# A retention recurrence and a gated feed-forward layer: order of the first chunk's transposes, second weight slices in halves, two states in a row

## The chip, the cores and the metric

The kernel runs on one core of a Trainium2 chip. The metric is the device time of the program in microseconds (us). Three runs of the kernel before took 225.05 to 225.13 us, with a median of 225.07 us. The profile is one execution of the same program; the span in it is 223.4 us, and all times "at" which something happens are counted from the start of that span. The TensorE clock that was granted is 1.0 throughout.

## The reference

For each of 4 batches and 8 heads a state of 64 x 64 decays and collects outer products, token by token, and the output of a token is its q times that state. The outputs of the 8 heads side by side are the 512 features x of a token. 3072 tokens then go through a gated feed-forward layer with 1536 hidden features:

```
for t in range(768):
    state = gamma * state + outer(k[t], v[t])      # per batch and head, gamma = 1 - 2**(-5-h)
    y[t]  = scale * q[t] @ state
x   = y as (4*768 tokens, 512)
out = (sigmoid(x @ w_gate) * (x @ w_val)) @ w_out
```

## The kernel before

**Chunks and tiles.** The 768 tokens are cut into 6 chunks of 128. One chunk of all 4 batches is a tile `t` of 512 columns for the feed-forward layer. Within a chunk the recurrence is worked out in closed form: scores (k times q), times a decay mask, times v; plus the q times the state that the chunks before have left. The attention works on pairs of batches: index `i` is chunk `i // 2`, pair `i % 2`, and `j` is the batch within the pair. "The last chunk" of the change's title means the last batch of the first token chunk, `(i, j) = (1, 1)`; "the third" is `(1, 0)`.

**Order.** The order on each engine is the order in which the code emits instructions (`manual_schedule`). The code first emits the loads of the first tile, then constants, then the head: the first tile's attention, with groups of matmuls on zeros in between (`keep_on`), then the first tile's feed-forward layer, then a loop over tiles 1 to 5 in which attention steps of later tiles are placed among groups of matmuls by a table, `plan`.

**Loads.** k, q, v and all weights are loaded by GpSimd's DMA queue, one instruction for each, in the order of the code; GpSimd also computes (`first_scaled`, line 371, `later_tables`, lines 182 and 184, `scale_k`, line 225), in the same order. `kf` and `qf`, the first batch's k and q, come over two other queues. Each of GpSimd's loads counts on one of 8 semaphores in turn, so a load is issued only when the one eight before it has landed. A weight slice `s` holds 256 of the 1536 hidden columns, that is two groups `n1 = 2s, 2s + 1` of 128. `load_w` (line 82) loads a slice whole (256 KB) or some of its 4 groups `kk` of 128 rows; the first slices of gate (`wg`) and val (`wv`) come in halves of rows, the others whole.

**The head.** `first_transpose(i, j, which, eng)` transposes k (`which` 0) or q (1) of one batch on TensorE and lets `eng` (ScalarE `act` or VectorE `dve`) copy it from PSUM to `kqT` (lines 348 and 349). `first_scores` (lines 233 and 355) multiplies them and masks the product on VectorE with `decay`, two instructions. `first_y` (lines 365 and 368) multiplies the masked scores by v and copies the result to `xT`. `exps_y(p)` (line 156) makes a quarter of `taby`, a table for later tiles, on ScalarE; it reads `col` and `lgz`, which VectorE makes (lines 159 and 153).

**The first feed-forward tile.** `first_parts` (line 410) computes two groups `n1` of gate or val, rows `kk` 0 and 1 of both groups first, then 2 and 3, so that it can begin with half a slice. `up_part` (line 392) computes one group with its four `kk` in a row. `gate_times_val` applies the sigmoid on ScalarE (line 420) and multiplies on VectorE (line 421). `first_state(i)` (line 379) forms the state of a pair from the scaled k (`ks`) and v, 16 matmuls of 64 columns in two halves of TensorE.

**Later tiles.** `xbar(i)` (line 220) transposes a pair's k and q by DMA from the queue of SyncE into `kqX`. `hold(i)` (line 540) is a tiny copy on GpSimd that waits for such a transpose, so that the loads behind it are not issued earlier. `block(old, new, st)` does one pair's outputs, the next one's scores and a state: `inter` (line 272), `quarter_scores` (line 249), `intra` (line 279), `state` (line 302). All matmul results use one ring of 8 PSUM banks (`bank`): the n-th result waits for the reader of the one eight before it.

Of the kernel before, what the change touches and what calls it, by code (L numbers as in the profile page):

```python
# [11 lines left out]
ALU = mybir.AluOpType  # L12
# [3 lines left out]
def kernel(  # L16
# [12 lines left out]
    nc = tc.nc  # L29
# [3 lines left out]
    C = 128  # L33
# [18 lines left out]
    def half(e):  # L52
        return slice(e * D, (e + 1) * D)
# [22 lines left out]
    wg = wpool.tile([128, KT, D_FF], BF16, name="wg")  # L76
    wv = wpool.tile([128, KT, D_FF], BF16, name="wv")
    wo = wpool.tile([128, NFF, D_MODEL], BF16, name="wo")

    def load_w(dst, w, s, kk=slice(0, KT)):  # L80
        cols = slice(s * 256, (s + 1) * 256)
        nc.gpsimd.dma_start(out=dst[:, kk, cols], in_=w.rearrange("(kk p) n -> p kk n", p=128)[:, kk, cols])  # L82

    def load_gate_val(s):
        load_w(wg, moe_w_gate, s)
        load_w(wv, moe_w_val, s)
# [7 lines left out]
    def first(dst, x, b, n, eng):  # L94
        eng.dma_start(out=dst, in_=x[b:b + n, :, 0:C, :].rearrange("b h s d -> s (b h) d"))  # L95
# [8 lines left out]
    def entry(t, j):  # L104
        return t[:, j * H:(j + 1) * H, :]
# [4 lines left out]
    ahead = const.tile([128, C], F32, name="ahead")  # L110
    first(entry(kn[0], 1), k, 1, 1, nc.gpsimd)
    nc.gpsimd.iota(ahead, pattern=[[-1, C]], base=0, channel_multiplier=1, allow_small_or_imprecise_dtypes=True)  # L112
    for x, b in ((q, 1), (k, 2), (q, 2), (k, 3), (q, 3), (v, 0), (v, 1), (v, 2), (v, 3)):
        tiles = kn if x is k else qn if x is q else vs
        first(entry(tiles[b // 2], b % 2), x, b, 1, nc.gpsimd)
    for dst, w in ((wg, moe_w_gate), (wv, moe_w_val)):
        load_w(dst, w, 0, slice(0, 2))
        load_w(dst, w, 0, slice(2, 4))
    load_gate_val(1)
    load_gate_val(2)  # L120


# [2 lines left out]
    nlg = const.tile([128, 2, NP], F32, name="nlg")  # L125
    lgz = const.tile([128, 2, NP], F32, name="lgz")
    lsc = const.tile([128, 1], F32, name="lsc")
    tok = const.tile([128, NT], F32, name="tok")
    col = const.tile([128, C], F32, name="col")
# [10 lines left out]
    nc.vector.memset(lsc, math.log(scale))  # L140
    for h in range(H):
        nc.vector.memset(nlg[:, h % 2, h // 2:h // 2 + 1], -lg[h])
    nc.vector.tensor_scalar(ident, ahead, 0.0, None, op0=ALU.is_equal)
    nc.vector.scalar_tensor_tensor(causal, ahead, -1.0e6, ahead, op0=ALU.mult, op1=ALU.min)
    for e in range(2):
        nc.vector.tensor_tensor(decay[:, e], causal.unsqueeze(1).to_broadcast([128, NP, C]),
                                nlg[:, e].unsqueeze(2).to_broadcast([128, NP, C]), op=ALU.mult)
        nc.scalar.activation(decay[:, e], decay[:, e], AX.Exp, bias=lsc)
    nc.vector.tensor_copy(entry(kn[0], 0), kf)
    nc.scalar.copy(entry(qn[0], 0), qf)  # L150
    for e in range(2):
        for j in range(2):
            nc.vector.tensor_scalar(lgz[half(e), j], nlg[half(e), e ^ j], -1.0, None, op0=ALU.mult)

    def exps_y(p):
        nc.scalar.activation(taby[:, p], col, AX.Exp, bias=lsc, scale=lgz[:, 0, p:p + 1])

    def later_constants():
        nc.vector.tensor_scalar(col, ahead, ahead[:, 0:1], -1.0, op0=ALU.subtract, op1=ALU.mult)
        for t in range(NT):  # L160
            nc.vector.tensor_scalar(tok[:, t:t + 1], ahead[:, 0:1], float(t * C), None, op0=ALU.add)

# [11 lines left out]
    def last_constants():  # L174
        nc.vector.tensor_scalar(causal, ahead, 0.0, None, op0=ALU.is_le)

    def later_tables():
        src = tabs.rearrange("s (p e) t -> s e t p", e=2)
        dst = tabsk.rearrange("s t j (p e) -> s j e t p", e=2)
        for j in range(2):  # L180
            for e in range(2):
                nc.gpsimd.tensor_copy(dst[:, j, e], src[:, e ^ j])
        for e in range(2):
            nc.gpsimd.tensor_tensor(maskk[:, e], causal.unsqueeze(1).to_broadcast([128, NP, C]),
                                    tabsk[:, 0, e, 0::2].unsqueeze(2).to_broadcast([128, NP, C]), op=ALU.mult)
# [5 lines left out]
    def zero_scores():  # L191
        for r in range(2):
            for j in range(2):
                for e in range(2):
                    nc.vector.memset(sts[r][j][e][half(1), :, 0:D], 0.0)
# [5 lines left out]
    def bank(shape, dt=F32):  # L201
        return pf.tile(shape, dt, tag="ff", name="ff")

    def heads(t, j, p):
        return t[:, j * H + 2 * p:j * H + 2 * p + 2, :].rearrange("s h d -> s (h d)")
# [80 lines left out]
    def x_of(t, kk, lo=0, hi=512):  # L286
        per = NP // len(xT[t])
        return xT[t][kk // per][:, kk % per, lo:hi]
# [17 lines left out]
    def new_za(i):  # L306
        za[i] = at.tile([128, 2, NP, D], F32, tag="za", name="za", bufs=4)
# [36 lines left out]
    def first_transpose(i, j, which, eng):  # L344
        x = (kn[i], qn[i])[which]
        tp = bank([128, NP, C], BF16)
        for p in range(NP):
            nc.tensor.transpose(tp[:, p, :], heads(x, j, p), ident)
        eng(kqT[i][:, which, j], tp)

    def first_scores(i, j):
        scores(i, j)
        for e, st in enumerate((stA, stB)):
            st[i, j] = at.tile([128, NP, C], BF16, tag=f"sf{e}", name=f"sf{e}", bufs=4)
            nc.vector.tensor_tensor(st[i, j], sc[i, j][e], decay[:, e], op=ALU.mult)
# [17 lines left out]
    def first_state(i):  # L373
        z = bank([128, 2, NP, D])
        for j in range(2):
            for p in range(NP):
                for e in range(2):
                    n = j * H + 2 * p + e
                    nc.tensor.matmul(z[half(e ^ j), j, p, :], ks[i][:, n, :], vs[i][:, n, :],  # L379
                                     start=(j == 0 and p == 0), stop=True, skip_group_check=True)  # L380
        new_za(i)
        nc.vector.tensor_copy(za[i], z)
# [11 lines left out]
    def up_part(t, w, n1s, lo=0, hi=512):  # L394
        n = hi - lo
        u = bank([128, 512])
        for i, n1 in enumerate(n1s):
            for kk in range(KT):
                product(t > 0, u[:, i * n:(i + 1) * n], w[:, kk, n1 * 128:(n1 + 1) * 128], x_of(t, kk, lo, hi),
                        start=(kk == 0), stop=(kk == KT - 1))  # L400
        return u[:, :len(n1s) * n]

    def first_parts(w, cuts):

        us = [bank([128, 512]) for _ in range(2)]
        for lo, hi in zip((0, *cuts), (*cuts, 512)):
            for k0 in (0, 2):
                for n1, u in enumerate(us):
                    for kk in range(k0, k0 + 2):
                        nc.tensor.matmul(u[:, lo:hi], w[:, kk, n1 * 128:(n1 + 1) * 128], x_of(0, kk, lo, hi),  # L410
                                         start=(lo == 0 and kk == 0), stop=(kk == KT - 1), skip_group_check=True)
        return us

    def gate_times_val(t, n1s, lo, hi, ps):
        n = hi - lo
        if t not in hT:
            hT[t] = ffn.tile([128, NFF, 512], BF16, tag="hT", name="hT", bufs=2)
        gs = ffn.tile([128, 512], F32, tag="gs", name="gs")
        g = gs[:, :len(n1s) * n]
        nc.scalar.activation(g, ps[0], AX.Sigmoid)  # L420
        nc.vector.tensor_tensor(hT[t][:, n1s[0]:n1s[-1] + 1, lo:hi], g.rearrange("p (i n) -> p i n", n=n),  # L421
                                ps[1].rearrange("p (i n) -> p i n", n=n), op=ALU.mult)
# [39 lines left out]
    def keep_on(n):  # L462
        u = bank([128, 512])
        for _ in range(n):
            nc.tensor.matmul(u, zero[:, :128], zero, start=True, stop=True)  # L465
# [3 lines left out]
    act, dve = nc.scalar.copy, nc.vector.tensor_copy  # L469

    new_kqT(0)
    new_kqT(1)
    keep_on(11)
    first_transpose(0, 0, 0, dve)
    first_transpose(0, 0, 1, act)
    later_constants()
# [1 line left out]
    first_scores(0, 0)  # L478
    more_constants()
    first_transpose(0, 1, 1, act)  # L480
    exps_y(0)
    first_transpose(1, 0, 0, act)
    exps_y(1)
    keep_on(1)
    first_scores(0, 1)
    first_transpose(1, 0, 1, act)
    exps_y(2)
    exps_y(3)
    keep_on(2)
    first_scores(1, 0)  # L490
    first_transpose(1, 1, 0, act)
    later_exps()
    first_transpose(1, 1, 1, dve)
    keep_on(2)
    first_y(0, 0, (act, act))
    first_scores(1, 1)
# [11 lines left out]
    first_scaled(1, 1, entry(kn[1], 1))  # L508
    load_gate_val(4)
    load_gate_val(5)  # L510
    for n1, ps in enumerate(zip(first_parts(wg, (3 * C,)), first_parts(wv, ()))):
        gate_times_val(0, (n1,), 0, 512, ps)
    for n1 in (2, 4):
        gates = [up_part(0, wg, (n1 + i,)) for i in range(2)]
        for i in range(2):
            gate_times_val(0, (n1 + i,), 0, 512, (gates[i], up_part(0, wv, (n1 + i,))))
        if n1 == 2:
            last_constants()
            zero_scores()
            later_tables()  # L520
        first_state(n1 // 2 - 1)
    load_out(0)
    load_out(1)
    load_kq(2)
# [105 lines left out]
```

## Time and profile before

| What | Value |
|---|---|
| time, median of three runs | 225.07 us (225.05 to 225.13) |
| span of the profiled run | 223.4 us |
| TensorE busy | 216.9 us, 97% |
| VectorE busy | 122.9 us, 55% |
| ScalarE busy | 70.2 us, 31% |
| GpSimd busy | 105.5 us, 47% |
| GpSimd's DMA queue (q0) | 80928 packets, 13.90 MB |

The engines are named PE (TensorE matmul), PEld (TensorE weight load), DVE (VectorE), ACT (ScalarE), POOL (GpSimd) and SP (SyncE). A line number such as L392 is that of the kernel's text, and can be the line of a helper that many steps share. A row of a timeline has the start, the time, the engine, the line, the operation, what is written and read, and the count; behind it stands how long the engine had been idle and what ended that. [...]consecutive matmuls overlap, so how fast TensorE goes is read from the distance of starts, not from durations.

Of the three parts of the head, by the profile's stretches: from 5.80 to 15.30 us TensorE is busy for 7.66 of 9.50 us, from 15.30 to 19.10 for 3.64 of 3.80 us, and from 19.10 to 27.00 for 7.84 of 7.90 us.

### The profile page before, as it was taken

To read this page: it belongs to the slowest core of one execution; us is meant where nothing else is said; L and a number is where in the kernel's file an instruction comes from. 1 tells how busy PE (TensorE), PEld (TensorE's weight loads), DVE (VectorE), ACT (ScalarE), POOL (GpSimd) and SP (SyncE) were. 2 spreads that over 40 slices of the span, in tenths; PEclk is the share of its full clock that TensorE was granted. 3 is DMA by queue.
4 is the path that set the end of the run, shared out by engine and by line. 5 is a ranking of instruction groups with operands and counts; after the bars stand their busy time and mean duration, and the time that the engine had idled before them with its cause. 6 is when DMAs were issued, how large, how long until landed. Compare 5 with 4: busy or idle time off the path is not lost.

```text
span 223.4 us, 6386 instructions
## 1 busy us (share of the span) xinstructions
PE 216.9 (97%) x2764; PEld 127.5 (57%) x2770; DVE 122.9 (55%) x243; ACT 70.2 (31%) x121; POOL 105.5 (47%) x128
## 2 busy tenths in 40 slices
PE   7799999999999999999999999999999999999994
PEld 2554444559999566556556556555555555555554
DVE  5862853094994885755916645925644922333301
ACT  5774232334233212332222332321332322333221
POOL 7999996878975916709367082640000000000000
PEclk9999999999999999999999999999999999999999
DMA  9999999999999999999999989896600012100022
GB/s 133 146 166 192 191 186 173 175 145 270 136 138 149 127 119 205 160 86 81 122 122 173 170 52 135 85 131 123 141 3 0 3 47 97 47 4 0 4 94 94
DMA packets 105788, 25.84 MB, mean 116 GB/s; under 512 B 94752, under 2 KB 102816, under 8 KB 105760
## 3 DMA queue, kind: packets, MB, share of 16 engines
q0 software_dynamic: 80928, 13.90, 85.3%
q1 hardware_dynamic: 23648, 11.21, 26.1%
q8 instruction: 21, 0.34, 0.6%
q10 hardware_dynamic: 1184, 0.33, 0.6%
q14 instruction: 7, 0.06, 0.1%
HBM read 28.31 MB, written 6.29 MB: 155 GB/s over the span
## 4 chain that ended last, share of the span: by engine, by line
PE 90%; POOL 5%; DMA 3%; issue 0%; DVE 0%; POOLq 0%
PE ff L392 82%; DMA wg<-in_moe_w_gate_dram 3%; PE ff L279 3%; PE ff L249 2%; POOL vs L95 2%; PE ff L272 2%; POOL kn L95 1%; POOL qn L95 1%; PE ff L302 1%; POOL wg L82 1%; POOL wv L82 1%; PE ff L214 0%; PE ff L379 0%; DVE ob L458 0%; POOL ahead L112 0%
## 5 line engine op out<-in xcount | busy, mean ns | idle before, releaser
L421 DVE TENSOR_TENSOR hT<-gs,ff 128x512 bf16<-128x512 f32 x72 | 48.6, 685 | 52.9 <-PE ff L392 49.9
L392 PE MATMUL ff<-xT,wg 128*64 128x512 bf16 (+2 forms) x616 | 71.9, 346 | 0.1
L392 PE MATMUL ff<-xT,wv 128*64 128x512 bf16 (+2 forms) x614 | 71.7, 346 | 0.1
L420 ACT ACTIVATE gs<-ff 128x512 f32<-128x512 f32 x72 | 42.9, 597 | 83.1 <-PE ff L392 82.7
L392 PE MATMUL ff<-wo,hT 128*64 128x512 bf16 (+3 forms) x580 | 64.6, 361 | 0.1
L392 PEld LDWEIGHTS <-wv 128*64 128x64 bf16 (+1 forms) x616 | 36.2, 109 | 24.4
L392 PEld LDWEIGHTS <-wg 128*64 128x64 bf16 (+1 forms) x616 | 35.5, 109 | 24.3 <-DMA wg<-in_moe_w_gate_dram 0.6
L392 PEld LDWEIGHTS <-hT 128*64 128x64 bf16 (+1 forms) x582 | 32.7, 109 | 27.1
L262 DVE TENSOR_TENSOR st<-ff,maskk 128x256 bf16<-128x256 f32 (+2 forms) x76 | 35.1, 492 | 7.5 <-PE ff L249 6.5
L442 ACT COPY ob<-ff 128x512 f32<-128x512 f32 x23 | 13.5, 585 | 57.0 <-PE ff L392 56.9
L295 DVE TENSOR_TENSOR xT<-ff,taby 128x512 bf16<-128x512 f32 x20 | 12.9, 685 | 23.7 <-PE ff L279 23.7
L540 POOL COPY held<-kqX 128x1 bf16<-128x1 bf16 x7 | 1.3, 184 | 34.9 <-DMA kqX<-qn 33.0
L225 POOL TENSOR_TENSOR ks<-kn,tabsk 128x1024 bf16<-128x1024 bf16 x8 | 15.5, 1942 | 1.6 <-PE ff L392 1.2
L70 POOL DMA_DIRECT2D qn<-in_q_dram x20 | 15.4, 795 | 0.0
L70 POOL DMA_DIRECT2D kn<-in_k_dram x20 | 15.2, 769 | 0.0
L60 POOL DMA_DIRECT2D vs<-in_v_dram x10 | 12.1, 1205 | 1.1 <-DMA wo<-in_moe_w_out_dram 1.0
L66 POOL DMA_DIRECT2D kn<-in_k_dram x10 | 9.3, 929 | 1.8 <-issue 1.7
L66 POOL DMA_DIRECT2D qn<-in_q_dram x10 | 9.2, 917 | 0.0
L465 PE MATMUL ff<-zero 128*128 128x512 bf16 x19 | 7.6, 527 | 1.2 <-DVE zero L139 1.2
L315 DVE TENSOR_TENSOR zb<-za,tabz 128x512 bf16<-128x512 f32 x10 | 8.2, 827 | 0.0
L279 PE MATMUL ff<-st,vs 128*64 128x128 bf16 x160 | 6.4, 222 | 0.0
L458 DVE COPY ob<-ff 128x256 f32<-128x256 f32 (+1 forms) x2 | 0.7, 357 | 9.2 <-PE ff L392 9.2
(74 smaller groups left out, 117.5 us busy)
## 6 DMA issues: line engine op xcount, KB each, us to landing
out_dram<-ob SPq DMA_DIRECT2D x23, 256.0 KB, 2.9
vs<-in_v_dram POOLq DMA_DIRECT2D x10, 256.0 KB, 7.5
kn<-in_k_dram POOLq DMA_DIRECT2D x13, 128.0 KB, 4.6
qn<-in_q_dram POOLq DMA_DIRECT2D x13, 128.0 KB, 4.6
wo<-in_moe_w_out_dram POOLq DMA_DIRECT2D x4, 384.0 KB, 7.0
wg<-in_moe_w_gate_dram POOLq DMA_DIRECT2D x5, 256.0 KB, 6.3
wv<-in_moe_w_val_dram POOLq DMA_DIRECT2D x5, 256.0 KB, 6.8
kn<-in_k_dram POOLq DMA_DIRECT2D x20, 64.0 KB, 4.0
```

The costliest lines, as they stand in the source:

```text
L60: nc.gpsimd.dma_start(out=vs[i], in_=v[2 * h:2 * h + 2, :, t * C:(t + 1) * C, :].rearrange("b h s d -> s (b h) d"))
L66: nc.gpsimd.dma_start(out=tiles[i][:, 0:H], in_=src[0])
L70: nc.gpsimd.dma_start(out=dst[:, e], in_=pairs[:, 1 - e])
L95: eng.dma_start(out=dst, in_=x[b:b + n, :, 0:C, :].rearrange("b h s d -> s (b h) d"))
L225: nc.gpsimd.tensor_tensor(ks[i], kn[i], tabsk[:, i // 2].rearrange("s j h -> s (j h)").unsqueeze(2) .to_broadcast([C, 2 * H, D]), op=ALU.mult)
L262: nc.vector.tensor_tensor(st[i, j][to, :, n], sc[i, j][e][of, :, n], maskk[to, e ^ j, :, n], op=ALU.mult)
L279: nc.tensor.matmul(y[i, j][half(e), p, :], vs[i][:, j * H + 2 * p + e, :], st[:, p, :], start=False, stop=True, skip_group_check=True)
L295: nc.vector.tensor_tensor(xT[t][0][:, :, c:c + C], y[i, j], taby, op=ALU.mult)
L392: nc.tensor.matmul(o[c], w[:, c], x, **marks)
L420: nc.scalar.activation(g, ps[0], AX.Sigmoid)
L421: nc.vector.tensor_tensor(hT[t][:, n1s[0]:n1s[-1] + 1, lo:hi], g.rearrange("p (i n) -> p i n", n=n), ps[1].rearrange("p (i n) -> p i n", n ...
L442: nc.scalar.copy(ob, o)
```

## The change

It has three parts.

1. *Head.* The k of the last batch is transposed ahead of the third batch's scores, not after them, so that its eviction doesn't stand in line with that of q; the eviction of its q moves from VectorE, where it comes after four masks, to ScalarE. To make room on ScalarE the four `exps_y` are spread differently, the first of them ahead of all evictions, for which VectorE makes `lgz` and `col` earlier.
2. *Weights.* The second slices of gate and val are loaded in halves of rows, like the first ones, and the groups 2 and 3 that use them go through `first_parts`, whose matmuls need only half a slice to begin.
3. *States.* The two `first_state` groups, which stood after groups 3 and 5, come one after the other after group 5.

```diff
--- before.py
+++ after.py
@@ -113,10 +113,10 @@
     for x, b in ((q, 1), (k, 2), (q, 2), (k, 3), (q, 3), (v, 0), (v, 1), (v, 2), (v, 3)):
         tiles = kn if x is k else qn if x is q else vs
         first(entry(tiles[b // 2], b % 2), x, b, 1, nc.gpsimd)
-    for dst, w in ((wg, moe_w_gate), (wv, moe_w_val)):
-        load_w(dst, w, 0, slice(0, 2))
-        load_w(dst, w, 0, slice(2, 4))
-    load_gate_val(1)
+    for n in range(2):
+        for dst, w in ((wg, moe_w_gate), (wv, moe_w_val)):
+            load_w(dst, w, n, slice(0, 2))
+            load_w(dst, w, n, slice(2, 4))
     load_gate_val(2)
 
 
@@ -140,23 +140,22 @@
     nc.vector.memset(lsc, math.log(scale))
     for h in range(H):
         nc.vector.memset(nlg[:, h % 2, h // 2:h // 2 + 1], -lg[h])
+    for e in range(2):
+        for j in range(2):
+            nc.vector.tensor_scalar(lgz[half(e), j], nlg[half(e), e ^ j], -1.0, None, op0=ALU.mult)
     nc.vector.tensor_scalar(ident, ahead, 0.0, None, op0=ALU.is_equal)
     nc.vector.scalar_tensor_tensor(causal, ahead, -1.0e6, ahead, op0=ALU.mult, op1=ALU.min)
     for e in range(2):
         nc.vector.tensor_tensor(decay[:, e], causal.unsqueeze(1).to_broadcast([128, NP, C]),
                                 nlg[:, e].unsqueeze(2).to_broadcast([128, NP, C]), op=ALU.mult)
         nc.scalar.activation(decay[:, e], decay[:, e], AX.Exp, bias=lsc)
+    nc.vector.tensor_scalar(col, ahead, ahead[:, 0:1], -1.0, op0=ALU.subtract, op1=ALU.mult)
     nc.vector.tensor_copy(entry(kn[0], 0), kf)
     nc.scalar.copy(entry(qn[0], 0), qf)
-    for e in range(2):
-        for j in range(2):
-            nc.vector.tensor_scalar(lgz[half(e), j], nlg[half(e), e ^ j], -1.0, None, op0=ALU.mult)
-
     def exps_y(p):
         nc.scalar.activation(taby[:, p], col, AX.Exp, bias=lsc, scale=lgz[:, 0, p:p + 1])
 
     def later_constants():
-        nc.vector.tensor_scalar(col, ahead, ahead[:, 0:1], -1.0, op0=ALU.subtract, op1=ALU.mult)
         for t in range(NT):
             nc.vector.tensor_scalar(tok[:, t:t + 1], ahead[:, 0:1], float(t * C), None, op0=ALU.add)
 
@@ -400,12 +399,12 @@
                         start=(kk == 0), stop=(kk == KT - 1))
         return u[:, :len(n1s) * n]
 
-    def first_parts(w, cuts):
+    def first_parts(w, n1s, cuts=()):
 
         us = [bank([128, 512]) for _ in range(2)]
         for lo, hi in zip((0, *cuts), (*cuts, 512)):
             for k0 in (0, 2):
-                for n1, u in enumerate(us):
+                for n1, u in zip(n1s, us):
                     for kk in range(k0, k0 + 2):
                         nc.tensor.matmul(u[:, lo:hi], w[:, kk, n1 * 128:(n1 + 1) * 128], x_of(0, kk, lo, hi),
                                          start=(lo == 0 and kk == 0), stop=(kk == KT - 1), skip_group_check=True)
@@ -471,6 +470,7 @@
     new_kqT(0)
     new_kqT(1)
     keep_on(11)
+    exps_y(0)
     first_transpose(0, 0, 0, dve)
     first_transpose(0, 0, 1, act)
     later_constants()
@@ -478,19 +478,18 @@
     first_scores(0, 0)
     more_constants()
     first_transpose(0, 1, 1, act)
-    exps_y(0)
+    exps_y(1)
     first_transpose(1, 0, 0, act)
-    exps_y(1)
+    exps_y(2)
     keep_on(1)
     first_scores(0, 1)
     first_transpose(1, 0, 1, act)
-    exps_y(2)
+    keep_on(2)
+    first_transpose(1, 1, 0, act)
+    first_scores(1, 0)
+    first_transpose(1, 1, 1, act)
     exps_y(3)
-    keep_on(2)
-    first_scores(1, 0)
-    first_transpose(1, 1, 0, act)
     later_exps()
-    first_transpose(1, 1, 1, dve)
     keep_on(2)
     first_y(0, 0, (act, act))
     first_scores(1, 1)
@@ -508,17 +507,18 @@
     first_scaled(1, 1, entry(kn[1], 1))
     load_gate_val(4)
     load_gate_val(5)
-    for n1, ps in enumerate(zip(first_parts(wg, (3 * C,)), first_parts(wv, ()))):
-        gate_times_val(0, (n1,), 0, 512, ps)
-    for n1 in (2, 4):
-        gates = [up_part(0, wg, (n1 + i,)) for i in range(2)]
-        for i in range(2):
-            gate_times_val(0, (n1 + i,), 0, 512, (gates[i], up_part(0, wv, (n1 + i,))))
-        if n1 == 2:
-            last_constants()
-            zero_scores()
-            later_tables()
-        first_state(n1 // 2 - 1)
+    for n1s in ((0, 1), (2, 3)):
+        gates = first_parts(wg, n1s, (3 * C,) if n1s[0] == 0 else ())
+        for n1, *ps in zip(n1s, gates, first_parts(wv, n1s)):
+            gate_times_val(0, (n1,), 0, 512, ps)
+    last_constants()
+    zero_scores()
+    later_tables()
+    gates = [up_part(0, wg, (n1,)) for n1 in (4, 5)]
+    for n1, gate in zip((4, 5), gates):
+        gate_times_val(0, (n1,), 0, 512, (gate, up_part(0, wv, (n1,))))
+    for i in range(2):
+        first_state(i)
     load_out(0)
     load_out(1)
     load_kq(2)
```

## The prediction

> **What bounds the kernel now.** I read the page first, then the chain of waits, then TensorE's own timeline, then the places where TensorE comes within 0.3 us of a transfer. The page gives TensorE 97% of the span and this chain:
>
> ```profile
> PE 90%; POOL 5%; DMA 3%; issue 0%; DVE 0%; POOLq 0%
> ```
>
> So the end is set by TensorE, except in a head of about 19 us. The chain of waits from 5 to 30 us shows what the head is:
>
> ```profile
> 6.91 3.50 POOL vs L95 x4
> 10.40 1.40 POOL wg L82 x2
> 11.80 1.32 POOL wv L82 x2
> 13.12 5.94 DMA wg<-in_moe_w_gate_dram
> 19.06 0.05 issue
> 19.10 3.63 PE ff L392 x16
> 22.73 0.37 PE ff L379 x16
> ```
>
> GpSimd issues one load after another, and the second gate slice (issued 13.12, landed 19.06) releases TensorE at 19.10. From there TensorE's timeline is closed. Its columns are start, duration, line, tiles, count, and the idle time before:
>
> ```profile
> 15.34 1.92 PE L410 MATMUL ff<-xT,wg 128*128 128x384 bf16 x16
> 17.31 1.68 PE L410 MATMUL ff<-xT,wv 128*128 128x512 bf16 x7
> 19.10 1.90 PE L392 MATMUL ff<-xT,wg 128*128 128x512 bf16 x8
> 20.84 1.89 PE L392 MATMUL ff<-xT,wv 128*128 128x512 bf16 x8
> 22.66 0.44 PE L379 MATMUL ff<-vs,ks 128*64 128x64 bf16 x16
> 23.04 1.90 PE L392 MATMUL ff<-xT,wg 128*128 128x512 bf16 x8
> ```
>
> Starts of 512-column matmuls lie 0.216 us apart. The last of the first val slice starts at 18.612, so the next could start at 18.828; it starts at 19.103. That hole is 0.275 us. The waits from 15 to 30 us name what weights were waited for:
>
> ```profile
> PEld L392 <- DMA wg<-in_moe_w_gate_dram: 0.6, 1, 0.6
> PEld L410 <- DMA wv<-in_moe_w_val_dram: 0.3, 1, 0.3
> ```
>
> The second of these cost TensorE nothing: the weights came at 17.951, and matmuls filled the time up to 17.958. But it is tight, which matters below.
>
> Then I looked for later places where TensorE meets a transfer. Two blocks of the attention run score matmuls (line 249) right after the state matmuls (line 272):
>
> ```profile
> 78.06 0.42 PE L272 MATMUL ff<-kqX,zb 64*64 64x128 bf16 x16
> 78.25 0.34 PEld L249 LDWEIGHTS <-kqX 64*64 64x64 bf16 x20
> 78.30 0.39 PE L249 MATMUL ff<-kqX 64*64 64x128 bf16 x16
> 78.36 2.65 SPq L220 DMA_TRANSPOSE kqX<-qn  x1
> ...
> 84.85 0.42 PE L272 MATMUL ff<-kqX,zb 64*64 64x128 bf16 x16
> 85.16 0.54 PEld L249 LDWEIGHTS <-kqX 64*64 64x64 bf16 x32
> 85.18 0.18 POOL L540 COPY held<-kqX 128x1 bf16<-128x1 bf16 x1 [6.25 <-DMA kqX<-qn]
> 85.19 0.65 PE L249 MATMUL ff<-kqX 64*64 64x128 bf16 x32
> ```
>
> In the block at 78 the scores follow the states after 0.247 us (78.303 less 78.056); in the block at 84.85 after 0.340 us. The transposed q of tile 6 was issued at 78.36 and took 6.7 us, so it landed at 85.06, and GpSimd's copy that waits for it starts in the same moment. **TensorE is already held there, by 0.09 us.** Whatever TensorE gains before 85 us stands in that queue unless that transfer comes earlier too.
>
> **What the skill says.** TensorEngine Tiling (Array Packing), Key Properties: changing the tiling mode drains TensorE. The trace agrees: from the last 128x128 matmul before a state group (22.352) to its first (22.661) are 0.309 us, not 0.216. DMA: Bandwidth & Descriptors, "Why a DMA increments its semaphore by 16 and not by 1": a load issued by GpSimd has landed only when all 16 engines have counted. The trace agrees: for the second half of the first val slice the first count comes at 15.94, the last at 17.91. Runtime: NRT & Kernel Launch, "Instruction fetch mechanics": instructions are refilled in 16 KiB blocks by the engine's own DMA queue. Queue q8 on the page has 21 packets in 0.34 MB, so 16 KB each; one starts at 15.51 and lasts 0.89 us.
>
> **Part 1, the attention head.** The states' tables: lgz (4 instructions, 0.95 us) moves into VectorE's idle 1.35 us before ident at 2.61: free. col (0.29 us, the next starts 0.20 later) moves ahead of the cast of k at 4.51; VectorE is free at 4.36, so the cast slips by 0.05 to 0.15 us, and the transpose behind it can't start before 5.86 anyway, when the eleven filling matmuls end. exps_y(0) (0.50 us) falls into ScalarE's idle 1.0 us before 6.92. On ScalarE an eviction is 0.58 us and a table 0.50, each following after 0.40 to 0.49. The k of the last chunk is then transposed at about 9.96, evicted from 10.53, so the order on TensorE becomes: third scores 10.70 (still released by the eviction of q at 10.07 + 0.58), transpose of q 11.03, its eviction by ScalarE 11.46 to 12.04 where VectorE did it from 12.32 to 12.74 behind four masks (2.66 us from 9.74). The first y moves from 12.01 to 11.78, the last scores from 12.79 to about 12.13: 0.66 us. Later_exps ends 0.2 us later than before, and ScalarE's first xT copies with it; nobody needs them before the gates. The banks stay eight apart with their readers done: I walked the ring, and no new reader is late. The chain then reaches the first gate matmul 0.6 us earlier than 15.34, but its weights land at 14.79 (issued 10.34, 4.45 us). So it starts at 14.83, 0.51 us earlier; 1.72 us of gate and 0.87 of val later it stands at 17.43 before the second half of the val slice, which landed at 17.91 (12.42 + 5.5). Nothing in the change touches an issue up to that one. **Part 1 is worth nothing past 17.95**, unless that late count moves. It is late because of stalled engines around the fetch at 15.51; TensorE's stream reaches that fetch about 0.5 us earlier, but its engine works its packets in turn, so I expect the same landing. Bounds: 0 to 0.5 us.
>
> **Part 2, halves of rows.** Two issues of 0.74 us each become four of 0.695 (10.34 to 13.12 for four). The data of a whole slice take about 1.36 us (20.37 less 19.06 and on), so the first half should land about 0.68 before 19.06, at 18.4, ahead of 18.83. With first_parts the eight matmuls of rows 0 to 1 come first and need the second half only at 19.69. The hole of **0.275 us** goes. The price: GpSimd's later issues move back by 4 x 0.695 - 2 x 0.737 = **1.31 us**. Behind them: slice 3 needed at 26.5 (landed 24.40), slice 4 at 29.9 (27.06), slice 5's val at 34.3 (32.51): all hold even 1.3 later, the last by 0.5. ks ends at 23.1 instead of 21.8, used at 25.8.
>
> **Part 3, two states in a row.** A state group costs 23.035 - 22.568 = 0.467 us; its eight pairs start 0.032 apart, 0.25 in all, so 0.21 is going in and coming out of the other tiling. In a row one such round trip goes: **0.21 us** (at least the 0.09 of the entry).
>
> **The sum.** TensorE is ahead by 0.275 + 0.21 = 0.48 us at 27 us. Two transfers stand in its way. The tile-2 q for the transposes at 38.80 was issued at 31.31 and took 7.3 us: landed 38.57. TensorE would be there at 38.32, so 0.25 is lost there unless it lands earlier. Then 85.19: no slack. The loads between 27 and 47 us take 6.5 to 8.6 us from issue to landing against 4.4 in the head, so they queue at the engines, and 1.31 us later issue mostly shortens the queue. From there to 85 each step waits for a landing, none for TensorE: tile 3's loads, its transpose, hold, tile 4's loads, and so on. So I take the landing at 85.06 as unmoved, and the gain is given back: within 0.1 of the time before, I say **225.0 us**.
>
> **The rivals.** (a) Held at 85.19, as above: 225.0, chance 0.42. (b) The gain gets through, because the transposed q of tile 6 lands at least 0.5 earlier (fewer stragglers among the engines when they are aligned by the later issues), or because the val half lands earlier as well: 225.07 - 0.48 = 224.6, down to 225.07 - 0.48 - 0.5 = 224.1. For it: landings that depend on a straggling engine can move by that much. Against: work done by the engines is the same. Chance 0.33. (c) The 1.31 us of GpSimd let engines run dry (slice 4, issued at 23.0 instead of 21.7, had only 5.4 us to landing, the shortest queue), the stream shifts, and tile 6's q lands up to 1.3 later: slower, 225.4 to 226.3, about 225.7. Chance 0.25.
>
> **The numbers.** (a) stays within 0.2% (0.45 us); of (b), 224.6 at its edge, some 0.04 too; of (c) 0.02. So faster 0.29, same 0.48, slower 0.23. The range runs from 224.3, into (b), to 226.0, into (c).
>
> **What would show it.** Right: last scores of the head near 12.1, first gates near 14.8, a wait for the val half until about 17.9, no hole at 18.8, states 0.25 us after each other, TensorE 0.4 to 0.5 ahead at 27 us, then a hole before line 249 of 0.5 us at 85 (part of it at 38.6). Wrong: no hole at 85 (then b), a landing of tile 6's q after 85.2 or any weight wait after 20 us (then c), a val half that lands well before 17.9.

## The result, and the profile after

The changed kernel takes 225.94 us (median of four runs, 225.69 to 226.14) against 225.06 us: a ratio of 1.0041, 95% interval 1.0023 to 1.0058. It is slower by 0.4%, which is the case that the prediction listed third, with a chance of 0.25. The profiled run is the quickest of the four, 225.69 us, with a span of 223.9 us; so its trace shows some 0.6 us of the 0.9. The time lies inside the range that was stated, but only because that range reached into the third case. Every ratio here is taken over all fast runs of both kernels, so it need not be the quotient of the two medians; two runs of experiment 7 and one of experiment 10, which took over 1.5% more than the fastest of their kernel, are left out of theirs.

The page's chain by engine shows in one line where the change went. TensorE had 90% of it before, GpSimd 5%:

```profile
PE 81%; POOL 14%; DMA 3%; issue 1%; DVE 0%; POOLq 0%
```

The chain of waits from 15 to 45 us, in the same columns as before (start, length, what), runs through GpSimd's instructions up to a load of q, and only then to TensorE. Before, it left GpSimd at 13.1 us:

```profile
14.64 1.41 POOL wv L82 x2
...
17.55 2.09 POOL ks L370 x2
19.65 0.69 POOL wg L82
20.33 0.75 POOL wv L82
21.08 2.09 POOL ks L370 x2
23.17 0.69 POOL wg L82
...
26.78 1.99 POOL maskk L183 x2
28.78 1.51 POOL wo L89 x2
...
32.68 6.83 DMA qn<-in_q_dram
39.52 0.05 issue
39.56 0.40 PE ff L213 x4
```

The load is tile 2's first q. Its landing releases the transposes of line 213 (214 before). TensorE's own timeline of the head:

```profile
14.93 0.82 PE L409 MATMUL ff<-xT,wg 128*128 128x384 bf16 x4
16.16 1.27 PE L409 MATMUL ff<-xT,wg 128*128 128x384 bf16 x12 [0.41 <-DMA wg<-in_moe_w_gate_dram]
17.49 1.67 PE L409 MATMUL ff<-xT,wv 128*128 128x512 bf16 x7
19.00 1.89 PE L409 MATMUL ff<-xT,wg 128*128 128x512 bf16 x8
20.72 1.89 PE L409 MATMUL ff<-xT,wv 128*128 128x512 bf16 x8
...
26.00 0.69 PE L378 MATMUL ff<-vs,ks 128*64 128x64 bf16 x32
26.62 1.04 PE L391 MATMUL ff<-xT,wg 128*128 128x512 bf16 x3
```

The three parts do what they are for. The first gates start at 14.93 instead of 15.34, there is no hole between the first val slice and the second gate slice, and the two states stand in one row of 32. Group 6 starts at 26.62, where it started at 26.97 before: TensorE is 0.35 us ahead. Group 6 and the transposes of tile 2 in the kernel before:

```profile
26.97 1.04 PE L392 MATMUL ff<-xT,wg 128*128 128x512 bf16 x4
...
38.63 0.39 PE L214 MATMUL ff<-ident,kn 128*128 128x128 bf16 x4
38.85 0.39 PE L214 MATMUL ff<-ident,qn 128*128 128x128 bf16 x4
```

In the changed kernel the timeline around 38 us shows TensorE losing three times its lead:

```profile
38.29 0.39 PE L213 MATMUL ff<-ident,kn 128*128 128x128 bf16 x4
39.20 0.88 POOL L66 DMA_DIRECT2D kn<-in_k_dram  x1
39.56 0.22 PEld L213 LDWEIGHTS <-qn 128*128 128x128 bf16 x4 [1.06 <-DMA qn<-in_q_dram]
39.56 0.40 PE L213 MATMUL ff<-ident,qn 128*128 128x128 bf16 x4 [0.89 <-DMA qn<-in_q_dram]
```

The transposes of k start 0.34 us earlier than before (38.29 against 38.63), those of q 0.71 later (39.56 against 38.85). Without a wait q follows k by 0.22 us, as it did before; here by 1.27. So 1.05 us are lost at one load. At 85 us TensorE is 0.82 us behind the kernel before, at its last matmul 0.59: it gets 0.22 back at 85 us, where the kernel before is held and the changed one isn't. These are its scores there, the counterpart of the row at 85.19 in the prediction:

```profile
85.91 0.52 PE L248 MATMUL ff<-kqX 64*64 64x128 bf16 x32
```

**The stream of loads.** The profile's stretches of 2 us give what the DMA engines moved, in the last column. First the kernel before, then the changed one:

```profile
24.00:26.00 2.00, 1.95 (x10) 0.89 (x10) 1.68 (x9) 1.19 (x2) 2.00 (x6) 1.00 1.45 194
26.00:28.00 2.00, 2.00 (x25) 0.93 (x23) 1.82 (x4) 0.00 (x0) 2.00 (x3) 1.00 1.43 185
28.00:30.00 2.00, 2.00 (x12) 0.88 (x9) 1.85 (x4) 0.83 (x2) 2.00 (x4) 1.00 1.33 176
30.00:32.00 2.00, 2.00 (x11) 0.94 (x10) 0.69 (x1) 0.87 (x2) 2.00 (x3) 1.00 1.19 184
```

```profile
24.00:26.00 2.00, 2.00 (x11) 0.75 (x10) 1.83 (x9) 0.71 (x2) 2.00 (x3) 1.00 1.06 127
26.00:28.00 2.00, 1.95 (x39) 1.25 (x40) 1.82 (x4) 0.30 (x1) 2.00 (x7) 1.00 1.39 178
28.00:30.00 2.00, 2.00 (x11) 0.90 (x10) 2.00 (x4) 0.87 (x2) 2.00 (x3) 1.00 1.23 156
30.00:32.00 2.00, 2.00 (x11) 0.87 (x9) 1.14 (x2) 0.62 (x2) 2.00 (x4) 1.00 1.27 186
```

Between 24 and 26 us the rate falls from 194 to 127 GB/s, and between 28 and 30 from 176 to 156. From 20 to 30 us the changed kernel moved 220 KB less than the kernel before, which at 194 GB/s is 1.1 us of its stream. The issue that came too late for the first dip is that of slice 4 (slices are counted from 0), at 23.03 instead of 21.68. GpSimd computes just ahead of it, first in the kernel before, then in the changed one:

```profile
19.66 2.14 POOL L371 TENSOR_TENSOR ks<-kn,tabs 128x512 bf16<-128x512 bf16 x2
21.68 0.81 POOL L82 DMA_DIRECT2D wg<-in_moe_w_gate_dram  x1
...
21.02 2.16 POOL L370 TENSOR_TENSOR ks<-kn,tabs 128x512 bf16<-128x512 bf16 x2
23.03 0.83 POOL L82 DMA_DIRECT2D wg<-in_moe_w_gate_dram  x1
```

The first w_out load is late by as much, 28.71 instead of 27.35, again behind GpSimd's computing (maskk, 2.0 us). The dip at 28 us is not its doing, though. Experiment 4 below issues w_out at 26.05 and keeps that dip; experiment 5 issues it at 28.65 and has none there. Their stretches, experiment 4 first:

```profile
28.00:30.00 2.00, 2.00 (x11) 0.88 (x9) 1.56 (x3) 0.60 (x2) 2.00 (x4) 1.00 1.18 145
30.00:32.00 2.00, 2.00 (x11) 0.93 (x10) 0.90 (x2) 0.60 (x1) 1.58 (x2) 1.00 1.37 197
...
28.00:30.00 2.00, 2.00 (x11) 0.88 (x9) 2.00 (x4) 0.61 (x2) 2.00 (x3) 1.00 1.40 191
30.00:32.00 2.00, 2.00 (x11) 0.92 (x10) 1.29 (x3) 0.60 (x1) 2.00 (x4) 1.00 1.11 153
```

What w_out's issue costs shows between 30 and 32 us: 153 GB/s in experiment 5, where it is late, 197 in experiment 4, where it is early. The kernel before has a dip of this kind of its own, 143 GB/s from 29.5 to 30.5 us. The dips at 24 and at 28 us shrink or go when slice 4 is issued earlier (experiments 5, 7 and 9). Why the same loads dip a second time, when slice 5 has been issued for over 2 us, stays open.

### The profile page after: what moved, and what is told of

Same layout as the page of the kernel before. It is cut to its first block, busy times and chain, and to the rows that moved or that the text cites. A ratio compares the mean times of both kernels' runs of the same rounds, so it can differ in the third digit from the quotient of the medians.

```text
span 223.9 us, 6389 instructions
## 1 busy us (share of the span) xinstructions
PE 217.2 (97%) x2765; PEld 127.5 (57%) x2770; DVE 123.0 (55%) x242; ACT 70.5 (31%) x122; POOL 106.9 (48%) x130
## 4 chain that ended last, share of the span: by engine, by line
PE 81%; POOL 14%; DMA 3%; issue 1%; DVE 0%; POOLq 0%
PE ff L391 74%; DMA qn<-in_q_dram 3%; PE ff L278 3%; POOL wg L82 2%; POOL wv L82 2%; POOL ks L370 2%; PE ff L248 2%; POOL vs L95 2%; PE ff L271 2%; POOL kn L95 1%; POOL qn L95 1%; PE ff L301 1%; POOL maskk L183 1%; POOL wo L89 1%; POOL kn L70 1%
## 5 line engine op out<-in xcount | busy, mean ns | idle before, releaser
L391 PE MATMUL ff<-xT,wv 128*64 128x512 bf16 (+2 forms) x608 | 70.0, 345 | 0.0
L391 PE MATMUL ff<-xT,wg 128*64 128x512 bf16 (+2 forms) x607 | 70.0, 346 | 0.1
L391 PEld LDWEIGHTS <-wv 128*64 128x64 bf16 (+1 forms) x608 | 35.4, 109 | 23.5
L391 PEld LDWEIGHTS <-wg 128*64 128x64 bf16 (+1 forms) x608 | 34.9, 109 | 23.2 <-DVE xT L294 0.2
L314 DVE TENSOR_TENSOR zb<-za,tabz 128x512 bf16<-128x512 f32 x10 | 9.0, 906 | 0.0
L82 POOL DMA_DIRECT2D wg<-in_moe_w_gate_dram x8 | 6.4, 820 | 0.0
```

What stands on the lines that cost most here:

```text
L391: nc.tensor.matmul(o[c], w[:, c], x, **marks)
```

## The experiments

Two theories stood at the start. **Issue:** GpSimd's later issue leaves the DMA engines without work, and what they then lose reaches tile 2's q. **Stragglers:** TensorE's changed order moves its instruction fetch among the loads, and some of the 16 engines fall behind in another way. In the table "issue" is that of slice 4's gate, "KB" what the stretches from 20 to 32 us add up to, "q" the landing of tile 2's first q, and "wait" the distance from the first transposes of k to those of q less the 0.22 us of work. All but the ratio are from the one profiled run of each kernel, in us. A load counts 16 times on its semaphore; its landing is the last of these counts, and they are read from the trace. Each experiment is compared with runs of the kernel before that were taken along with it, so the time of that kernel differs a little from one to another.

| Kernel | issue | KB | q | wait | ratio to before, 95% interval |
|---|---|---|---|---|---|
| before | 21.68 | 2260 | 38.57 | 0 | |
| changed | 23.03 | 2044 | 39.52 | 1.05 | 1.0041 (1.0023 to 1.0058) |
| changed, slices whole | 21.94 | 2310 | 37.98 | 0 | 0.9995 (0.9979 to 1.0010) |
| before, slices in halves | 23.03 | 2032 | 39.29 | 0.53 | 1.0054 (1.0036 to 1.0072) |
| before, one more scaling on GpSimd | 23.22 | 2010 | 40.15 | 1.26 | 1.0034 (1.0018 to 1.0051) |
| changed, tables moved on GpSimd | 23.04 | 2012 | 39.52 | 1.35 | 1.0065 (1.0045 to 1.0084) |
| changed, slice 4 first | 20.94 | 2106 | 39.08 | 0.90 | 1.0026 (1.0011 to 1.0041) |
| changed, tables on VectorE | 23.05 | 2010 | 39.02 | 0.78 | 1.0043 (1.0025 to 1.0061) |
| changed, both of these two | 21.01 | 2164 | 38.67 | 0.14 | 0.9995 (0.9979 to 1.0012) |

**1. Part 2's loads undone.**

```diff
-    for n in range(2):
-        for dst, w in ((wg, moe_w_gate), (wv, moe_w_val)):
-            load_w(dst, w, n, slice(0, 2))
-            load_w(dst, w, n, slice(2, 4))
+    for dst, w in ((wg, moe_w_gate), (wv, moe_w_val)):
+        load_w(dst, w, 0, slice(0, 2))
+        load_w(dst, w, 0, slice(2, 4))
+    load_gate_val(1)
```

> The changed kernel with the second slices loaded whole again, so GpSimd issues as early as before (parts 1 and 3 stay, and groups 2 and 3 still go through first_parts). Theory 'issue' (GpSimd's 1.31 us of later issue let the DMA engines run dry, and tile 2's q lands too late for its transposes): tile 2's first q lands at 38.2 to 38.7, the wait in front of its transposes is 0.3 us or less, no dry stretch at 24 us; time 224.7 to 225.1. Theory 'stragglers' (TensorE runs ahead, its instruction fetch falls elsewhere, and the landings of all later loads shift with it): q lands at 39.4 or later, wait 0.8 to 0.9, time 225.6 to 226.1.

Measured 225.00 us against 225.16. TensorE's order is that of the changed kernel, and the loss is gone: q at 37.98, no wait. This speaks for the issue and against the stragglers. (Parts 1 and 3 stay in this kernel, and no gain of theirs shows.)

**2. Part 2's loads alone.** The same lines the other way round, in the kernel before.

> The kernel before with nothing but the second slices in halves of rows. Theory 'issue': slices 4 and 5 and all behind them are issued 1.3 us later, the engines run dry near 24 and 28 us, tile 2's first q lands at 39.3 to 39.6, TensorE waits 0.5 to 0.9 us for it; time 225.6 to 226.0. Theory 'stragglers': TensorE's order is the one of before, so q lands near 38.6 and the time is 225.0 to 225.1.

225.93 us against 225.16: the whole loss with TensorE's old order. q landed at 39.29, at the edge of what was expected. Of the 0.89 us that this kernel's profile is behind at its last matmul, 0.53 are lost at q; another 0.6 go between 60 and 75 us, whose cause isn't settled, and 0.22 come back at 85 us.

That halves move more slowly is not seen: in the changed kernel the first counts of the four halves of slice 1 lie 0.67 to 0.72 us apart, those of the two whole loads of slice 2 behind them 1.3 and 1.4.

**3. The delay alone.**

```diff
     first_scaled(0, 0, kf)
+    first_scaled(0, 0, kf)
```

> The kernel before with the first of GpSimd's four scalings of k done twice (the same values, one more instruction of 1.19 us, each following after 1.02), so that every later issue on GpSimd is about 1.0 us later and no transfer is changed. Theory 'issue': tile 2's first q lands 0.5 to 0.8 later than before, near 39.2, TensorE waits 0.3 to 0.6 us for it; time 225.4 to 225.8. Theory 'stragglers', and likewise a theory that the halves themselves move slower: 225.0 to 225.1.

225.91 us against 225.16. No transfer is changed, no slice is halved, and one more instruction on GpSimd costs the kernel 0.34%. The profile's waits of TensorE from 30 to 100 us hold one line:

```profile
PE ff L214 <- DMA qn<-in_q_dram: 1.1, 1, 1.1
```

The delay was larger than intended: slice 4 is issued 1.54 us later than before, 1.26 of it from the added instruction and 0.27 because GpSimd's loads were late from the start in this profile. So q came at 40.15 and not near 39.2, and the time is a little above the 225.4 to 225.8 that were expected; the profiled run took 226.24 us, more than its median. No load is added here, so it isn't the number of loads either.

**4. Which issue is the late one? The tables moved.** GpSimd's tables behind tile 2's loads bring w_out forward.

```diff
     zero_scores()
-    later_tables()
 ...
     load_kq(2)
+    later_tables()
```

> The changed kernel with GpSimd's tables (tabsk and maskk, 2.7 us of its work) moved behind the loads of tile 2's k and q, so that the loads of w_out, k and q are issued 2.7 us earlier than in the changed kernel; nothing else moves. Theory 'issue': the first w_out load is issued near 26.0, the dry stretch at 28 us goes (that at 24 stays), tile 2's first q lands by 38.3, no wait or one under 0.2 us in front of its transposes; time 224.5 to 225.1, the latter if the transpose of tile 6's q at 85 us then holds TensorE as the prediction has it. Theory 'stragglers': q lands at 39 or later and the time stays at 225.6 to 226.1.

A miss: 226.68 us against 225.16. By the medians it is slower than the changed kernel; the intervals of the two ratios overlap. GpSimd's timeline shows what happened:

```profile
26.05 1.54 POOL L89 DMA_DIRECT2D wo<-in_moe_w_out_dram  x2
...
31.28 0.76 POOL L70 DMA_DIRECT2D qn<-in_q_dram  x1 [0.42 <-DMA wg<-in_moe_w_gate_dram]
33.69 0.74 POOL L70 DMA_DIRECT2D qn<-in_q_dram  x1 [1.65 <-DMA wv<-in_moe_w_val_dram]
...
35.10 2.04 POOL L183 TENSOR_TENSOR maskk<-causal,tabsk 128x512 f32<-128x512 f32 x2
37.09 1.57 POOL L89 DMA_DIRECT2D wo<-in_moe_w_out_dram  x2
```

w_out is issued 2.7 us earlier, yet its first count comes at 33.35 us (33.31 in the changed kernel): the engines were late already from slice 4, whose first count came at 26.59 (26.57 in the changed kernel, 25.45 before). So w_out's issue alone isn't the cause. And the tables now stand ahead of w_out's third part, issued at 37.09 instead of 35.04, which moves the chain of later loads. TensorE's waits from 30 to 100 us:

```profile
PE ff L248 <- DMA kqX<-qn: 1.3, 1, 1.3
PE ff L213 <- DMA qn<-in_q_dram: 1.2, 1, 1.2
```

The first of them is tile 6's transposed q, which landed at 87.14: the place where the prediction saw TensorE held.

**5. Slice 4 first.**

```diff
+    load_gate_val(4)
     first_scaled(1, 0, entry(kn[1], 0))
     first_scaled(1, 1, entry(kn[1], 1))
-    load_gate_val(4)
```

> The changed kernel with one exchange on GpSimd: the fourth weight slices are issued ahead of the second pair of scalings of k, not behind them, so that slice 4 is issued near 21.0 us (23.0 in the changed kernel, 21.7 before) and the second pair of scalings ends near 24.6, still ahead of its use at 25.8. Theory 'issue at slice 4' (the engines run dry near 24 us because slice 4 is issued too late, and all later landings carry it): no dry stretch at 24 us, tile 2's first q lands by 38.7, the wait in front of its transposes is 0.3 us or less; time 224.6 to 225.1. Theory 'issue at w_out' (the late issue at 28.7 us does it): q lands at 39.4 and the time is 225.7 or more; the run with the tables moved already speaks against it.

225.72 us against 225.18: too slow for the theory as I had put it. The time falls into the range of its rival (225.7 or more), q at 39.08 into neither; and the ratio isn't clear of the changed kernel's. The stretch from 24 to 26 us moves 157 GB/s instead of 127, but the one from 30 to 32 now falls to 153 (186 in the changed kernel): the dry place has moved to w_out, still issued at 28.65, whose first count stays at 33.28.

**6. Tile 2's loads in the order of use.** The first half of q ahead of the second half of k, nothing else.

> The changed kernel with tile 2's six k and q loads in the order of their use: first half of k, first half of q, then the four others. Nothing is issued earlier as a whole. If the landing of tile 2's first q is what costs the changed kernel its time: that q lands about 1.1 us earlier, near 38.4, the wait of 0.9 us in front of its transposes goes to under 0.2, TensorE stays 0.2 to 0.4 us ahead of the kernel before up to 85 us, and then waits up to 0.5 us for the transposed q of tile 6, which lands as in the changed kernel near 85.2; time 225.0 to 225.4. If the stream is late as a whole and the wait only moves to the next load: a wait of 0.5 us or more before line 213 or at w_out, time 225.7 to 226.1.

225.81 us against 225.18 (1.0026, 1.0012 to 1.0040): the second branch. Its profiled run was a long one, 227.27 us; in it TensorE waits before loads of w_out, k and q between 37 and 43 us and again for tile 6's transposed q. This is what a stream that is late as a whole would do; it rests on that one profile.

**7. Both 5 and 6.**

> Both of these changes on the changed kernel: slice 4 ahead of the second pair of scalings, and tile 2's k and q in the order of use. Theory 'issue at slice 4': q lands near 37.5, no wait at the transposes, TensorE 0.3 to 0.5 us ahead of the kernel before until 85 us; time 224.5 to 224.9 where the transpose of tile 6's q lands by 84.9, up to 225.1 where it lands near 85.1. The rival that the halves cost more than issue (transfers themselves slower): 225.3 or more.

225.40 us against 225.18 (1.0018, 0.9998 to 1.0038). Not what I had expected: the time falls to the rival. What speaks against slower halves are experiment 3, where nothing is halved, and the first counts given with experiment 2. Whether the two together are better than either isn't shown, as the intervals overlap; w_out is still issued at 28.66, its first count still at 33.23.

**8. Tables on VectorE.** The six instructions go from GpSimd to VectorE, after group 8.

> The changed kernel with the tables on VectorE alone. Theory 'two dry places': the stretch at slices 3 and 4 stays, so tile 2's first q lands at 39.0 to 39.5 as with the tables moved behind the loads, TensorE waits 0.6 to 1.1 us; but GpSimd has 2.7 us less to do, so tile 6's transpose isn't late: time 225.3 to 225.8. If w_out's late issue alone were the cause: q by 38.4, time 224.4 to 224.8.

225.75 us against 225.06: as "two dry places" has it. Slice 4 is issued at 23.05, w_out at 26.06, and w_out's first count stays at 33.33. The dip at 28 us stays too, at 144 GB/s.

**9. Both dry places mended,** 5 and 8 together.

> The changed kernel with both stretches of late issue mended: slice 4 ahead of the second pair of scalings, and GpSimd's tables (tabsk, maskk) made by VectorE after group 8 instead, so that the first w_out load is issued near 26.0 and nothing on GpSimd stands between the weights and w_out. Theory 'two dry places' (each of the two alone left the other: slices 3 and 4 issued too late, and w_out issued too late): the first count of w_out comes near 32.2 instead of 33.3, tile 2's first q lands by 38.3, no wait over 0.2 us at its transposes; time 224.3 to 224.8. If it is a loss that no issue order mends: 225.4 or more.

225.11 us against 225.06, and with 0.9995 against 1.0041 the loss of the changed kernel is gone: the intervals of the two ratios don't touch. Three stretches of its profile, for the same columns as above:

```profile
24.00:26.00 2.00, 2.00 (x10) 0.78 (x8) 1.92 (x9) 0.78 (x2) 2.00 (x3) 1.00 1.32 168
26.00:28.00 2.00, 2.00 (x40) 1.19 (x39) 1.98 (x4) 0.23 (x1) 2.00 (x4) 1.00 1.34 181
28.00:30.00 2.00, 2.00 (x11) 0.94 (x10) 2.00 (x4) 0.87 (x2) 2.00 (x4) 1.00 1.43 182
```

No dip under 168 GB/s is left, w_out's first count comes at 32.48 and q lands at 38.67, not by 38.3 as expected. The gain of 0.2 to 0.7 us on the kernel before that I expected on top didn't come. In its profiled run TensorE lost part of its lead at slice 2, which landed at 22.46, 0.9 later than in the changed kernel's profile, though issued at the same time.

**10. Part 1 alone.**

> The kernel before with part 1 alone (the head's order, the q of the last batch to ScalarE, the tables' spread). The last scores of the head come 0.4 to 0.7 us earlier, the first gates about 0.5 earlier (when their weights land near 14.8). By the prediction all of it is lost at the second half of the first val slice and then at the second gate slice, which lands near 19.06: TensorE at 27 us as before, time 225.0 to 225.2. If the head's order moves a landing (gate's second half later, as in two of the profiles, or val's earlier): up to 0.3 us either way.

225.11 us against 225.06, a ratio of 1.0000 (0.9983 to 1.0017). Nothing, as predicted. Its profile shows the loss: 0.3 us of wait for the second gate slice, until 19.31. In it TensorE is 0.21 us behind the kernel before at 27 us, GpSimd's weight loads being 0.27 late from the start, and level after 85 us.

**11. Part 3 alone.**

> The kernel before with part 3 alone, the two states in a row. One round trip between the tilings goes: TensorE is 0.21 us ahead at 27 us (bounds 0.09 and 0.25). No GpSimd issue moves. If tile 2's q (landed 38.57) and tile 6's transposed q (landed 85.06) hold TensorE as the prediction has it, it is all given back and the time is 225.0 to 225.2, equal to before; if neither holds it in most runs, 224.8 to 224.95.

224.83 us against 225.18, a ratio of 0.9983 (0.9968 to 0.9998), the only kernel here whose interval lies wholly below the time of the kernel before, if barely. TensorE's timeline:

```profile
26.27 0.69 PE L379 MATMUL ff<-vs,ks 128*64 128x64 bf16 x32
26.90 1.04 PE L392 MATMUL ff<-xT,wg 128*128 128x512 bf16 x4
```

Of the 0.21 us only 0.07 are left at group 6 (26.90 against 26.97), because the groups ahead of it started later in this profile. It ends 0.28 ahead: the other 0.22 come at 85 us, where tile 6's transposed q landed at 84.22 and held nothing. So this one profile doesn't show where the median's 0.35 us come from.

**12. Part 3 and the tables on VectorE, slices whole.** 

> The kernel before with part 3 and the tables on VectorE, weights whole: GpSimd is 2.7 us ahead at w_out, so there is no late issue at all. If the late landings of tile 2 and tile 6 still cost the runs of 'states only' something: 224.3 to 224.7. If the loads behind are limited by the engines and no longer by issue: as with states only, 224.8.

225.12 us against 225.06 (1.0000, 0.9982 to 1.0018), which is neither of the two that were expected. No gain of earlier loads is seen: tile 2's q landed at 38.12 as in experiment 11. Whether the tables cost VectorE's other work something isn't settled; the two intervals overlap.

## Why the prediction was wrong

- **The step that failed** is "they queue at the engines, and 1.31 us later issue mostly shortens the queue". The 1.31 us were right (slice 4 came 1.35 later). The queue was mis-sized, in two ways. The 6.5 to 8.6 us belong to loads behind slice 4, but the delay meets slice 4 first. And I read the queue from issue to landing, and a landing is the last of 16 counts. Slice 4 before had 5.4 us to its last count, but 3.77 to its first (21.68 to 25.45), and the shortest that any weight load of the head has to its first count in that profile is 3.45. So, as an estimate, the engines that were ahead had about 0.3 us of work in store, and of the 1.31 us some 1.0 had to go through to what comes behind; tile 2's q came 0.95 later. In the changed kernel slice 3 came down to 3.57 (19.45 to 23.02) and slice 4 to 3.54. The engines that lagged did have work, and slice 4's last count was as early as before, 27.04 against 27.06. But its first count was 1.1 us later (26.57 against 25.45), first and last now lay 0.5 us apart instead of 1.6, and the loads behind landed 0.4 to 1 us later. Experiments 1 to 3 show the cause from three sides; 9 shows that the loss goes when slice 4 and w_out are both issued earlier.
- **Where the store went.** Before, from the second half of the first val slice on, the loads had 3.52, 4.14, 4.88, 5.51 and 6.10 us from issue to first count: a whole slice takes 0.74 us to issue and 1.3 to 1.5 to move, so the queue grows with each. In the changed kernel the four halves have 3.49, 3.48, 3.49 and 3.47: a half takes 0.695 to issue and about 0.68 to move, so the queue doesn't grow until the whole slices behind them (4.14, 4.70). When GpSimd turns to scaling k, the queue is 1.4 us shorter.
- **The rival (c)** named this mechanism and put it at 225.4 to 226.3; I gave it 0.25, and looked for its effect at tile 6's q. It came at tile 2's q, where I had counted 0.25 us of wait; it was 1.05. (The 0.25 was reckoned from 38.80; the transposes of q start at 38.85.) Of the signs for (c), no weight wait came after 20 us, and tile 6's q landed at 85.24, just past the 85.2.
- **The hold at 85 us** is real but wasn't reached: with TensorE 0.82 us behind, the scores followed the states after 0.25 us, without a wait. It was also more than the 0.09 us that I read: in the kernel before the 32 score matmuls of that block take 0.65 us, in the changed one, not held, 0.52. 0.09 and 0.13 are the 0.22 us that the changed kernel gets back there. "Unmoved" was nearly right: tile 6's q landed at 85.24, not 85.06. But in experiment 4 it came at 87.14 and held TensorE for 1.3 us, and in experiments 1 and 8 to 12 at 83.9 to 84.3, so the landing isn't as fixed as I took it.
- **Part 1** is worth nothing, as predicted (experiment 10), though not by the steps given. In the changed kernel's profile the last scores start at 12.38 and not 12.13, and the val half landed at 17.12 and not 17.91. It was the second half of the gate slice that held TensorE until 16.16: its first count came at 14.59 as before (14.52), its last at 16.12 instead of 15.43. "I expect the same landing" failed both ways. The instruction fetch of queue q8, at 15.51 before, was at 13.77. In eleven of the fourteen profiles the largest step by which a last count falls back behind its first, among the loads up to 17 us, is at a load whose first count lies within 1 us of the start of that fetch; in three (experiments 3, 5 and 9) another load has a larger one. So the fetch is likely a cause of such steps, and not the only one; no run moved it by itself.
- **Part 2's hole** of 0.275 us went, but TensorE came there at 19.00, not 18.83, so 0.10 us of it was gained.
- **Part 3's 0.21 us** was right: from where group 6 could have started (last val matmul of group 5 at 25.688, plus 0.216) to where it did (26.62) are 0.72 us, against twice 0.467 before: 0.21 saved. The Trainium skill's TensorEngine Tiling (Array Packing), Key Properties, says that a change of tiling mode drains TensorE; this is what one such round trip costs here.
- **The sum** at 27 us was 0.35 us ahead instead of 0.48, the difference being the gate half.

## What to carry to other kernels

A load that is split in two costs its issuing engine nearly a whole issue more, and what the queue cannot absorb of that delay goes to the loads behind it. Read how much queue there is from issue to the *first* count of a load, not to its landing: here the engines that were ahead ran dry first. A queue grows only while a load takes longer to move than to issue; the halves here took as long for the one as for the other. Before loads are split or an instruction is added on the engine that issues them, look for the places where that engine computes between two issues, and move the computing behind the issues. Here the loss went when two such places were mended together, and neither alone was clear of it.

## What the runs showed of the hardware that was not expected

- Half a slice costs GpSimd nearly as much issue as a whole one: 0.695 us against 0.737.
- The last of the 16 counts wanders from run to run where the first doesn't: for the second half of the first gate slice the first count lies between 14.31 and 14.64 in all the profiles told of here, the last between 15.22 and 16.56. The runs of the kernel before spread from 224.4 to 227.0 us in the experiments, so a gain of 0.2 us needs many runs to be seen; how much of that spread comes from late counts wasn't tested.
